# Two-layer decode step on one core: one load for the output weights of two head pairs, two pieces for the last values, four pieces for the last down weights

## Chip, cores and metric

One core of one Trainium2 chip. The metric is the device time of one execution in microseconds (us). A run is one execution.

## The reference

Two identical layers (the same weights) of attention and a gated MLP, for one token:

```python
x = x + A(layernorm(x)); x = x + B(layernorm(x))      # layer 0
x = x + A(layernorm(x)); x = x + B(layernorm(x))      # layer 1
# A: 32 heads of 192, keys and values: the last 4096 of 32768 positions, D = 640
#    q = x @ wq; p = softmax(q k^T * 192**-0.5); A = (p v) @ wo
# B: g = x @ w_gate; u = x @ w_up; B = (sigmoid(g) * u) @ w_down,  F = 1536
```

All inputs are bfloat16. The work is matrix times vector, so each byte of keys, values and weights is used once per layer, and the kernel is a stream of loads with a little computing beside it.

## The kernel before

The heads are handled in 16 pairs. For a pair, the host lays the projection weights and the keys in one unit ("a") and the values and the output weights in another ("b"); slots in on-chip memory hold 7 units. A list `seq` gives the order of the loads; all go out on one queue (SP), and each waits until the slot it writes is free. PE runs its instructions in order.

What the change touches, with cuts:

```python
WFIN = [(0, 6), (6, 10), (10, 12)]           # last down weights: chunks of each piece
def last_values(l, p):                       # last pair of a layer: values in three pieces
    return [("b1", l, p), ("b0", l, p, 0), ("b0", l, p, 1)]
seq = ... + [("a", 0, 15), ("b", 0, 14)] + last_values(0, 15)
seq += [("wol", 14), ("wol", 15)] + [(k,) for k in (*MW, *MV)] + ...   # MW: pieces of the MLP's weights
...
seq += [("fg",), ("fu",), ("fd", 0), ("fd", 1), ("fd", 2)]             # last MLP's weights
...
# down-weight pieces d0, d1 of layer 0's MLP overwrite gate pieces, so they are issued
# only after the gate projection has read those:
MAFTER = {"d0": ("wg0",), "d1": ("wg1",), ...}
...
# end of layer 0's attention (p = 15), in PE's order:
PVmm(p, 1)          # probabilities times values
RS(1, 2)            # row sums
PVn(p - 1, 0)       # output weights of pair 14: 15 matmuls, waits for load "wol14"
PVt(1, False)       # transpose pair 15's output: 6 matmuls, then one DVE operation
PVn(p, 1)           # output weights of pair 15: 15 matmuls, waits for load "wol15"
...
# the end of the kernel: each chunk of down weights is four matmuls on four column groups
for i_, (c0, c1) in enumerate(WFIN):
    for c in range(c0, c1):
        for g in range(NRG): matmul(yrow[32*g : 32*g+1, 0:RW], lhsT=hT[:, c:c+1], rhs=...)
```

## Time and profile before

| | |
|---|---|
| time, 3 runs | 515.14 us median (514.93 to 515.77) |
| span of the profiled run | 513.6 us |
| loads, read from the trace's packet records | 66 DMAs of 128 packets, 218.63 MB |
| last byte of weights landed | 510.72 us of the span |

From the profile's page, kernel before: the span; the DMA engines' busy share in tenths and the GB/s in 40 slices of the span; the queue of the loads (packets, MB, share of 16 engines' span); the chain that ended last by engine.

```profile
span 513.6 us, 8573 instructions
...
DMA  9999999999999999999999999999999999999996
GB/s 430 425 422 425 426 429 439 451 443 425 429 425 434 426 443 451 435 425 429 411 416 417 410 438 435 433 425 427 453 443 434 434 429 429 426 430 423 426 427 276
...
q1 hardware_dynamic: 9512, 218.63, 99.1%
...
DMA 63%; PE 24%; DVE 7%; ACT 2%; SPq 2%; issue 2%; DVEq 0%; POOL 0%; ACTq 0%; POOLq 0%
```

The DMA engines are full in every slice but the last, and most of the chain is DMA. PE, busy 51% on the page, waits for loads. A gain must come from the stream or from what follows its last byte. One weakness of the busy share: a packet that takes longer than usual counts as busy for all of its time. Slices 20 to 23 (about 244 to 295 us) show 410 to 417 GB/s, where the others but the last show 422 to 453, and the share does not show it.

The end of layer 0's attention, kernel before, from the timeline. Columns: start us, duration us, engine, line, operation, output<-input, shape, count, and in brackets the idle time before and what ended it. L502 applies output weights, L488 transposes, L377 is the residual sum that ends the attention, L212 issues loads.

```profile
271.20 0.54 PE L502 MATMUL bank<-sh,big 128*128 128x1 bf16 x15
...
271.80 0.30 PE L488 MATMUL bank<-cst,o_sb 128*128 128x1 bf16 x6
272.13 0.22 DVE L491 TENSOR_SCALAR sh<-bank,sc 128x3 bf16<-128x3 f32 x1 [0.48 <-PE bank L488]
...
272.63 0.56 PE L502 MATMUL bank<-sh,big 128*128 128x1 bf16 x15 [0.54 <-DMA big<-in_uc_dram]
273.23 0.16 DVE L377 SCALAR_TENSOR_TENSOR sc<-bank,sc 128x5 f32<-128x5 f32 x1 [0.87 <-PE bank L502]
...
274.95 0.90 SPq L212 DMA_DIRECT2D big<-in_wd_dram  x2
```

Pair 14's weights are applied at 271.20, then pair 15's output is transposed, and only then does PE wait 0.54 us, for pair 15's weights. The first down-weight load of the MLP is issued at 274.95.

The chain of waits at the end, kernel before (start us, duration us, what):

```profile
486.16 24.89 DMA big<-in_wd_dram
...
511.09 0.46 PE o L719 x7
...
511.57 0.33 DVE o_sb L725
```

The long DMA entry is the last load, issued at 486 us behind everything else. After it there are 0.46 us of matmuls and then the cast of the result.

### The profile page before, as it was taken

The numbers are of one execution on the slowest core, as the hardware profiler recorded it, in microseconds if no ns is written. First come the engines' busy times: TensorE is split into PE (matmuls) and PEld (weight loads), VectorE is DVE, ScalarE is ACT, GpSimd is POOL, SyncE is SP. The second block draws the span as 40 slices with busy tenths as digits, with TensorE's granted clock in tenths as the row PEclk, the third lists the DMA queues.
The fourth block names the chain that finished last, engine by engine and source line by source line (L and its number), as shares of the span: only waits on it lengthen the run. The fifth ranks groups of instructions, "written<-read, shape, count | busy, mean of one in ns | idle before, by whom it ended". The sixth has DMA issues, their size and how long they took to land.

```text
span 513.6 us, 8573 instructions
## 1 busy us (share of the span) xinstructions
PE 263.4 (51%) x3716; PEld 137.6 (27%) x3716; DVE 99.2 (19%) x376; ACT 85.2 (17%) x171; POOL 4.2 (1%) x31
## 2 busy tenths in 40 slices
PE   0462456344643265345566767864625245634665
PEld 0221222122311132222234434432312122212334
DVE  0221212112211121111121333231202112210311
ACT  0110111011110111011120033130301011101220
POOL 0010000000000000000000000000000000000000
PEclk9955665565566755566575568676857555556655
DMA  9999999999999999999999999999999999999996
GB/s 430 425 422 425 426 429 439 451 443 425 429 425 434 426 443 451 435 425 429 411 416 417 410 438 435 433 425 427 453 443 434 434 429 429 426 430 423 426 427 276
DMA packets 9676, 218.97 MB, mean 426 GB/s; under 512 B 1208, under 2 KB 1208, under 8 KB 4664
## 3 DMA queue, kind: packets, MB, share of 16 engines
q1 hardware_dynamic: 9512, 218.63, 99.1%
q8 instruction: 13, 0.21, 0.1%
q10 hardware_dynamic: 144, 0.06, 0.0%
q14 instruction: 7, 0.06, 0.0%
HBM read 218.69 MB, written 0.00 MB: 426 GB/s over the span
## 4 chain that ended last, share of the span: by engine, by line
DMA 63%; PE 24%; DVE 7%; ACT 2%; SPq 2%; issue 2%; DVEq 0%; POOL 0%; ACTq 0%; POOLq 0%
DMA big<-in_uc_dram 54%; PE scores L410 8%; PE o L467 7%; DMA big<-in_wd_dram 6%; DVE sc L420 3%; DMA big<-in_wu_dram 3%; PE bank L426 2%; SPq L212 2%; PE bank L395 2%; PE bank L502 1%; ACT e_sb L434 1%; PE bank L440 1%; ACT diag L423 1%; DVE sc L452 1%; DVE qs L398 1%
## 5 line engine op out<-in xcount | busy, mean ns | idle before, releaser
L410 PE MATMUL scores<-big,qs 128*32 128x512 bf16 x744 | 81.5, 605 | 9.9 <-DVE qs L398 9.9
L395 PE MATMUL bank<-sh,big 128*128 128x1 bf16 x465 | 17.1, 166 | 133.0 <-DMA big<-in_uc_dram 130.7
L467 PE MATMUL o<-big,et_sb 128*2 128x384 bf16 x1024 | 78.7, 474 | 5.9 <-DMA big<-in_uc_dram 3.4
L423 ACT ACTIVATE diag<-cst,sc 128x128 f32<-128x128 bf16 x32 | 12.8, 402 | 307.5 <-DVE sc L420 299.4
L420 DVE TENSOR_REDUCE sc<-scores 128x1 f32<-128x1024 f32 x31 | 38.0, 1225 | 79.2 <-PE scores L410 79.2
L395 PEld LDWEIGHTS bank<-sh,big 128*128 128x128 bf16 x465 | 14.6, 103 | 136.2 <-DMA big<-in_uc_dram 113.4
L426 PE MATMUL bank<-diag,sc 128*128 128x128 f32 x64 | 22.5, 447 | 47.9 <-ACT diag L423 47.9
L434 ACT ACTIVATE e_sb<-scores,sc 128x1024 bf16<-128x1024 f32 x31 | 37.4, 1205 | 41.8 <-DVE sc L429 39.5
L467 PEld LDWEIGHTS o<-big,et_sb 128*2 128x2 bf16 x1024 | 28.0, 108 | 43.8 <-issue 31.1
L398 DVE TENSOR_TENSOR qs<-bank,cst 128x96 bf16<-128x96 f32 x31 | 8.0, 258 | 162.4 <-PE bank L395 162.4
L410 PEld LDWEIGHTS scores<-big,qs 128*32 128x32 bf16 x744 | 23.7, 131 | 43.0 <-issue 29.6
L426 PEld LDWEIGHTS bank<-diag,sc 128*128 128x128 f32 x64 | 14.1, 274 | 73.0 <-ACT diag L423 71.5
L474 ACT CAST o_sb<-o 128x384 bf16<-128x384 f32 x64 | 29.8, 474 | 22.5 <-PE o L467 22.3
L502 PE MATMUL bank<-sh,big 128*128 128x1 bf16 x480 | 17.2, 165 | 15.2 <-DVE sh L491 14.6
L444 DVE CAST et_sb<-bank 128x64 bf16<-128x64 f32 x32 | 7.2, 225 | 71.8 <-PE bank L440 71.8
L502 PEld LDWEIGHTS bank<-sh,big 128*128 128x128 bf16 x480 | 14.5, 99 | 17.7 <-DVE sh L491 12.1
L427 DVE TENSOR_REDUCE sc<-bank 128x2 f32<-128x128 f32 x32 | 9.3, 292 | 42.1 <-PE bank L426 42.1
L440 PE MATMUL bank<-cst,e_sb 128*128 128x8 bf16 x256 | 11.7, 169 | 6.8 <-ACT e_sb L434 6.7
L440 PEld LDWEIGHTS bank<-cst,e_sb 128*128 128x128 bf16 x256 | 8.9, 101 | 22.9 <-issue 16.4
L450 PE MATMUL o<-sc 128*128 128x2 f32 x62 | 14.0, 295 | 0.6 <-ACT o_sb L474 0.6
L450 PEld LDWEIGHTS o<-sc 128*128 128x128 f32 x62 | 12.1, 243 | 1.9 <-ACT o_sb L474 1.3
L452 DVE RECIPROCAL sc<-o 64x1 f32<-64x1 f32 x62 | 10.2, 164 | 9.5 <-PE o L450 7.8
(76 smaller groups left out, 106.4 us busy)
## 6 DMA issues: line engine op xcount, KB each, us to landing
big<-in_uc_dram SPq DMA_DIRECT2D x20, 7104.0 KB, 22.6
big<-in_uc_dram SPq DMA_DIRECT2D x12, 3552.0 KB, 21.2
big<-in_uc_dram SPq DMA_DIRECT2D x1, 3072.0 KB, 21.5
big<-in_uc_dram SPq DMA_DIRECT2D x4, 768.0 KB, 11.6
big<-in_uc_dram SPq DMA_DIRECT2D x5, 480.0 KB, 6.9
big<-in_uc_dram SPq DMA_DIRECT2D x1, 2048.0 KB, 10.7
big<-in_uc_dram SPq DMA_DIRECT2D x1, 2016.0 KB, 10.6
big<-in_wg_dram SPq DMA_DIRECT2D x4, 480.0 KB, 14.7
```

The source lines that it names most:

```text
L395: ins = t.matmul(qe[:, i:i + 1], lhsT=slot(sa, c * 2 * DH + c0, P), rhs=xq[:, c:c + 1], start=(c == 0), stop=(c == DC - 1))
L410: ins = t.matmul(sc_x[1 + b][32 * j:32 * j + 32, :], lhsT=qs[:, y, k, :], rhs=slot(sa, WQE + k * W + (4 * b + j) * 512, 512), start=(k == ...
L420: pg.op("dve", lambda v: v.reduce_max(out=mx, in_=sc_x[0][:], axis=AX.X), wr=[res("mx")], ex=sc_x[3:5])
L423: pg.op("act", lambda a: a.mul(out=diag[:], in_=ident, mul=mx), rd=[res("cst"), res("mx")], wr=[res("diag")])
L426: pg.op("pe", lambda t: t.matmul(dmx[:, 0:P], lhsT=ones_f, rhs=diag[:], start=True, stop=True), rd=[res("diag"), res("ones")], ex=[rb[2]])
L434: pg.op("act", lambda a: a.activation(out=e_sb[:], in_=sc_x[0][:], func=ACT.Exp, bias=nbias, scale=srs_c, accum_out=rowsum), rd=[res("nbia ...
L440: ins = t.matmul(qe[:, 0:2 * NB].rearrange("p (r x) -> p r x", r=2)[:, :, 4 * b:4 * b + 4], lhsT=e_sb[:, b * P:(b + 1) * P], rhs=sel, star ...
L450: pg.op("pe", lambda t: t.matmul(sm, lhsT=ones_f, rhs=rs2[z], start=True, stop=True), rd=[res(f"rs2{z}"), res("ones")], wr=[res("rsum")], ...
L452: rb[bk].last["dve"] = pg.op("dve", lambda v, h=h: v.reciprocal(out=Rn[z][64 * h:64 * h + 64], in_=sm[64 * h:64 * h + 64, h:h + 1]), rd=[r ...
L467: ins = t.matmul(o8[h][32 * j:32 * j + 2, 0:2 * DH].rearrange("p (a d) -> p a d", a=2), lhsT=et_sb[:, z, h * NB + 2 * u:h * NB + 2 * u + 2 ...
L474: pg.op("act", lambda a, h=h: a.copy(out=o8_sb[:, :, h * DH:(h + 1) * DH], in_=o8[h][:, 0:2 * DH].rearrange("p (a d) -> p a d", a=2)), wr= ...
L502: ins = t.matmul(yT[:, j:j + 1], lhsT=wo[:, c * D + j * P:c * D + (j + 1) * P], rhs=oTb[z][:, c:c + 1], start=False, stop=(c == 2), skip_g ...
```

## The change

The intent: fewer, longer loads in the stream, and less work after the last byte. Output weights of pairs 14 and 15 get a buffer of their own and land as one row across the border of two neighbouring slots. Of the last values of a layer, the second head and half of the first come as one load, the last quarter follows. The last down weights come in four pieces, the last with one chunk instead of two.

```diff
-    WFIN = [(0, 6), (6, 10), (10, 12)]
+    WFIN = [(0, 6), (6, 10), (10, 11), (11, 12)]
     def last_values(l, p):
-        return [("b1", l, p), ("b0", l, p, 0), ("b0", l, p, 1)]
+        return [("b1", l, p), ("b0", l, p)]
-    seq += [("wol", 14), ("wol", 15)] + ...
+    seq += [("wol",)] + ...
-            pg.dma(q_dma(slot(s, NB * DH, o1 - NB * DH), b_in(it[2], NB * DH, o1)), f"b1_{it[1]}", wr=[rslot[s]])
+            pg.dma(q_dma(slot(s, NHALF, o1 - NHALF), b_in(it[2], NHALF, o1)), f"b1_{it[1]}", wr=[rslot[s]])
-            pg.dma(q_dma(slot(s, o, WOE), b_in(it[1], o, o + WOE)), f"wol{it[1]}", ...)
+            pg.dma(q_dma(big[:, PLACE[s] * UNIT + wo_at(15):PLACE[s] * UNIT + UNIT + WOE], wl_d), "wol", ...)
-                for part in (0, 1) if half and h == 0 else (None,):
+                for part in (1, 0) if half and h == 0 else (None,):
-                rw = [rslot[sv], res(f"wol{p}")]
+                rw = [rslot[sv], res("wol")]
... (waits and start/stop flags of the split values, the list entries of the last down weights, and the host's layout of the new buffer, are cut)
```

Bytes and matmuls stay the same; 66 loads become 64.

More of the change, by code (lines that the diff above doesn't have):

```diff
@@ L108, in decode_kernel @@
 def decode_kernel(ctx: ExitStack, nc, cx: bass.AP, uc: bass.AP,
-                  wg_d: bass.AP, wu_d: bass.AP, wd_d: bass.AP, out: bass.AP):
+                  wg_d: bass.AP, wu_d: bass.AP, wd_d: bass.AP, wl_d: bass.AP, out: bass.AP):
     scale = float(DH) ** -0.5
@@ L225, in last_values @@
     def last_values(l, p):
-        return [("b1", l, p), ("b0", l, p, 0), ("b0", l, p, 1)]
+        return [("b1", l, p), ("b0", l, p)]
     seq = [("a", 0, 0)] + [("c", 0, p) for p in range(1, 15)] + [("a", 0, 15), ("b", 0, 14)] + last_values(0, 15)
-    seq += [("wol", 14), ("wol", 15)] + [(k,) for k in (*MW, *MV)] + [("a0", 0), ("wom",), ("a0", 1), ("a0", 2), ("a", 1, 3), ("b", 1, 2)]
+    seq += [("wol",)] + [(k,) for k in (*MW, *MV)] + [("a0", 0), ("wom",), ("a0", 1), ("a0", 2), ("a", 1, 3), ("b", 1, 2)]
     seq += [("b", 1, 3), ("a", 1, 4), ("b", 1, 4), ("a", 1, 5), ("a", 1, 6), ("b", 1, 5)]
     seq += [("c", 1, p) for p in range(7, 13)] + [("a", 1, 13), ("b", 1, 12)] + last_values(1, 13)
-    seq += [("fg",), ("fu",), ("fd", 0), ("fd", 1), ("fd", 2)]
+    seq += [("fg",), ("fu",), *(("fd", i) for i in range(len(WFIN)))]
     seq_pos = [0]
@@ L284, in try_load @@
             s = B_SLOT[it[1]][it[2]]
-            o = it[3] * NHALF
-            pg.dma(q_dma(slot(s, o, NHALF), b_in(it[2], o, o + NHALF)), f"bh{it[3]}", wr=[res(f"bh{it[3]}")], extra=ev_done["b1"])
+            pg.dma(q_dma(slot(s, 0, NHALF), b_in(it[2], 0, NHALF)), "bh0", wr=[res("bh0")], extra=ev_done["b1"])
         elif k == "a0":
@@ L294, in try_load @@
         elif k == "wol":
-            s = B_SLOT[0][it[1]]
-            o = wo_at(it[1])
-            pg.dma(q_dma(slot(s, o, WOE), b_in(it[1], o, o + WOE)), f"wol{it[1]}", wr=[res(f"wol{it[1]}")], extra=ev_done["b1" if it[1] == 15 else "b14"])
+            s = B_SLOT[0][15]
+            assert PLACE[B_SLOT[0][14]] == PLACE[s] + 1 and wo_at(15) + WOE == UNIT and wo_at(14) == 0
+            pg.dma(q_dma(big[:, PLACE[s] * UNIT + wo_at(15):PLACE[s] * UNIT + UNIT + WOE], wl_d), "wol", wr=[res("wol")], extra=ev_done["b1"] + ev_done["b14"])
         elif k in MW:
@@ L460, in PVmm, with f @@
                 vt = (mreg(h * NB * DH, NB * DH) if inm else slot(sv, v_at(p) + h * NB * DH, NB * DH)).rearrange("p (t d) -> p t d", t=NB)
-                for part in (0, 1) if half and h == 0 else (None,):
+                for part in (1, 0) if half and h == 0 else (None,):
                     us = range(NB // 2) if part is None else range(part * NB // 4, (part + 1) * NB // 4)
-                    def f(t, h=h, vt=vt, us=us):
+                    first = range(NB // 4, NB // 4 + 4) if part is not None else range(4)
+                    final = range(NB // 4 - 4, NB // 4) if part is not None else range(NB // 2 - 4, NB // 2)
+                    def f(t, h=h, vt=vt, us=us, first=first, final=final):
                         for u in us:
@@ L467, in f @@
                             ins = t.matmul(o8[h][32 * j:32 * j + 2, 0:2 * DH].rearrange("p (a d) -> p a d", a=2), lhsT=et_sb[:, z, h * NB + 2 * u:h * NB + 2 * u + 2],
-                                           rhs=vt[:, 2 * u:2 * u + 2, :], start=(u < 4), stop=(u >= NB // 2 - 4), tile_position=(0, 32 * j))
+                                           rhs=vt[:, 2 * u:2 * u + 2, :], start=u in first, stop=u in final, tile_position=(0, 32 * j))
                         return ins
-                    rV = rc if inm else [rslot[sv]] + ([] if part is None else [res(f"bh{part}")]) if half else [rval[sv]]
+                    rV = rc if inm else [rslot[sv]] + ([res("bh0")] if part == 0 else []) if half else [rval[sv]]
                     ev = pg.op("pe", f, rd=[res(f"et{z}")] + rV, ex=[rb[4 + h]])
@@ L897, in _layout @@
     cx[:, C_X:] = x.reshape(DC, P).T
-    return dict(cx=cx, uc=uc, wg=blk(wg), wu=blk(wu), wd=wdn)
+    wl = np.concatenate([wo[n * 2 * DH:(n + 1) * 2 * DH].reshape(P, WOE) for n in (NPAIR - 1, NPAIR - 2)], axis=1)
+    return dict(cx=cx, uc=uc, wg=blk(wg), wu=blk(wu), wd=wdn, wl=wl)
 def kernel(**inputs):
```

## The prediction

> **What bounds the kernel.** The DMA stream. The page shows DMA at 9 tenths in every slice but the last, q1 at 99.1% of 16 engines' span, 426 GB/s; PE is busy 51%. The trace's packet records show no hole in q1 from about 2 us after the span's start until the last down weights. Their durations are very regular: 2,560 B 102 ns, 3,840 B 149, 7,680 B 291, 56,832 B 2,098. From these I estimate 27.2 B/ns per engine plus 8 ns per packet; a DMA also has a 9 ns semaphore packet. 27.2 x 16 = 435 GB/s, which the Trainium skill ("DMA: Bandwidth & Descriptors", "Where 436 GB/s comes from") gives as the port ceiling: the trace agrees. So only the packets' fixed part and the tail after the last byte can be saved; the bytes do not change.
>
> **The stream.** Removed: one DMA of last values per layer (2), one of output weights (1). Added: one of down weights. Net -2 DMAs, each costing an engine 8 packets x 8 ns + 9 ns = 73 ns (estimate): -0.15 us. The new 1,280 B packets should take 55 ns, by the same line. (The same page, "Why small descriptors are slow", names a fixed overhead per packet; the trace agrees in kind, with 8 ns.)
>
> **The tail.** In the trace the last piece's eight matmuls run as two waves of four, from 511.09 and 511.18 us; the cast follows at 511.57 (the chain of waits puts 0.46 us on them). With one chunk last there is one wave, 0.29 us per matmul: -0.15 us. Cast, output DMA and clears stay.
>
> **What gets worse but should be hidden.** In layer 0, PE, which is in order, applies the weights of pair 14 before it transposes pair 15's output. Now both pairs wait for one DMA, which lands when that of pair 15 did (PE idle 0.54 us on a DMA before the last 15 matmuls at 272.63, in the timeline). So pair 14's 0.55 us, the transposes' 0.3 us and DVE's 0.22 us come after the landing: layer 0's attention ends about 1.1 us later. That delays the first projections, and the issue of the first two down-weight pieces. Those start moving 2.75 and 3.85 us after issue; the kernel's first load needed 1.0. So about 1.7 us of slack takes 1.1 us of delay, and the projection then catches up (it idles 0.6 us per piece on landings). The last values: h=1 and half of h=0 (24 matmuls, about 1.3 us) start when the larger piece lands and end before the last quarter lands, some 1.8 us later; eight matmuls follow that, as before. In layer 1 the final weights are already queued, so nothing of this is on the chain.
>
> **Prediction.** 515.14 - 0.15 - 0.15 = about 514.8 us, range 514.2 to 515.4. Faster by over 2%: 0.005; within 2%: 0.985; slower: 0.01.
>
> **What would show it right.** Span about 0.3 us shorter; no hole in q1 at 275 to 285 us; 1,280 B packets near 55 ns; one wave of four matmuls between last landing and cast; layer 0's residual about 1 us later, with no effect on the end.
>
> **What would make it wrong.** The 1.1 us delay exceeds the slack and opens a hole in the stream (up to +1 us); small last packets land late; one DMA engine runs behind the others by another amount (the last piece starts over 2.7 us apart on different engines); or scatter (514.93 to 515.77 before) hides it all.

## The result, and the profile after

| | before | after |
|---|---|---|
| median of 6 runs each | 515.03 us (514.58 to 515.87) | 514.71 us (514.58 to 516.82) |
| ratio | | 0.9997, 95% interval 0.9979 to 1.0015 |

A ratio is the mean time of one kernel's runs over that of the other's of the same rounds, so it is not quite the ratio of the medians. The two kernels are the same at this resolution. Five of the six runs after lie between 514.58 and 514.75; the sixth, 516.82, is the one that was profiled.

The page's lines of that long run after, which answer those of before:

```profile
span 515.4 us, 8570 instructions
...
DMA  9999999999999999999999999999999999999996
GB/s 424 428 420 423 429 428 454 441 428 423 428 429 437 446 432 437 423 437 428 422 416 393 382 443 427 425 433 434 453 424 437 437 428 428 446 428 411 433 423 275
...
q1 hardware_dynamic: 9224, 218.63, 99.0%
...
DMA 64%; PE 24%; DVE 7%; ACT 2%; issue 2%; SPq 1%; DVEq 0%; ACTq 0%
```

The same lines of a short profiled run of the same kernel (514.57 us, from the experiments below, run again2):

```profile
span 513.3 us, 8570 instructions
...
DMA  9999999999999999999999999999999999999996
GB/s 426 430 422 425 422 435 430 447 447 430 430 425 425 439 425 434 452 438 434 402 415 413 413 439 438 428 433 434 440 430 452 438 430 425 435 430 421 427 429 276
...
q1 hardware_dynamic: 9224, 218.63, 99.2%
```

All DMA shares are alike. The long run differs in slices 22 and 23 (about 270 to 296 us), where the rate falls to 393 and 382 GB/s. These slices hold the MLP of layer 0.

The end of layer 0's attention, after, short run (L503 is before's L502, L489 before's L488, L376 before's L377):

```profile
272.55 0.54 PE L503 MATMUL bank<-sh,big 128*128 128x1 bf16 x15 [1.27 <-DMA big<-in_wl_dram]
...
272.95 0.30 PE L489 MATMUL bank<-cst,o_sb 128*128 128x1 bf16 x6
273.29 0.22 DVE L492 TENSOR_SCALAR sh<-bank,sc 128x3 bf16<-128x3 f32 x1 [1.61 <-PE bank L489]
...
273.57 0.56 PE L503 MATMUL bank<-sh,big 128*128 128x1 bf16 x15 [0.32 <-DVE sh L492]
274.17 0.16 DVE L376 SCALAR_TENSOR_TENSOR sc<-bank,sc 128x5 f32<-128x5 f32 x1 [0.66 <-PE bank L503]
...
275.90 0.81 SPq L212 DMA_DIRECT2D big<-in_wd_dram  x2
```

and three of these instructions in the long run:

```profile
273.31 0.51 PE L503 MATMUL bank<-sh,big 128*128 128x1 bf16 x15 [2.34 <-DMA big<-in_wl_dram]
...
274.89 0.17 DVE L376 SCALAR_TENSOR_TENSOR sc<-bank,sc 128x5 f32<-128x5 f32 x1 [0.64 <-PE bank L503]
...
276.62 0.80 SPq L212 DMA_DIRECT2D big<-in_wd_dram  x2
```

PE now waits on the row before pair 14's weights, and transposes, DVE and pair 15's weights follow one after the other behind that landing. The residual starts at 274.17 in the short run, 0.94 us later than before, and the first down-weight load is issued 0.95 us later. In the long run they are 1.66 and 1.67 us later than before.

The end of the chain of waits, long run after:

```profile
487.96 24.98 DMA big<-in_wd_dram
...
512.98 0.33 PE o L720 x4
...
513.34 0.32 DVE o_sb L726
```

Four matmuls, 0.33 us, stand where 0.46 us stood.

Three readings used below come from the trace's records, not from a view.
- The *lead* of the first down-weight load (piece d0 of layer 0's MLP) is the time from the start of its issue to the start of its first data packet. The Trainium skill ("Perfetto Trace Analysis", DMA Instruction, HWDGE) says that a DMA instruction's interval does not contain the movement of data; the trace agrees (two issues took 0.90 us together, and the first packet came 2.75 us after the first began), so the packets must be looked at.
- The *loss* at 270 to 300 us is, over all packets of the load queue, the duration beyond what a packet of its size usually takes, plus the time with fewer than 16 packets in flight, divided by 16 engines. It depends a little on how such packets are counted: a second count by these words gave 0.07 to 0.15 us more for every profile, with nearly the same ranking. Splits of the loss by time, below, are from the second count.
- The *period* is the time from the start of one packet to the start of the next on one engine, after sorting the packets to engines by size and by gapless succession.

### The profile page after: what moved, and what is told of

Read it like the earlier page. It is cut to its first block, busy times and chain, and to the rows that moved or that the text cites. A ratio compares the mean times of both kernels' runs of the same rounds, so it can differ in the third digit from the quotient of the medians. Undisturbed runs are those within 1.5% of the kernel's fastest.

```text
span 515.4 us, 8570 instructions
## 1 busy us (share of the span) xinstructions
PE 261.4 (51%) x3716; PEld 137.3 (27%) x3716; DVE 99.4 (19%) x376; ACT 84.7 (16%) x171; POOL 4.2 (1%) x31
## 3 DMA queue, kind: packets, MB, share of 16 engines
q1 hardware_dynamic: 9224, 218.63, 99.0%
## 4 chain that ended last, share of the span: by engine, by line
DMA 64%; PE 24%; DVE 7%; ACT 2%; issue 2%; SPq 1%; DVEq 0%; ACTq 0%
DMA big<-in_uc_dram 54%; PE scores L409 8%; PE o L468 7%; DMA big<-in_wd_dram 6%; DMA big<-in_wu_dram 4%; DVE sc L419 3%; PE bank L425 2%; PE bank L394 2%; PE bank L503 1%; SPq L212 1%; ACT diag L422 1%; ACT e_sb L433 1%; PE bank L439 1%; DVE sc L451 1%; DVE qs L397 1%
## 5 line engine op out<-in xcount | busy, mean ns | idle before, releaser
L409 PE MATMUL scores<-big,qs 128*32 128x512 bf16 x744 | 82.7, 612 | 10.0 <-DVE qs L397 9.9
L468 PE MATMUL o<-big,et_sb 128*2 128x384 bf16 x1024 | 75.7, 463 | 3.8 <-DMA big<-in_uc_dram 2.8
L468 PEld LDWEIGHTS o<-big,et_sb 128*2 128x2 bf16 x1024 | 27.6, 106 | 39.8 <-issue 30.0
L503 PE MATMUL bank<-sh,big 128*128 128x1 bf16 x480 | 17.2, 165 | 17.7 <-DVE sh L492 15.3
L503 PEld LDWEIGHTS bank<-sh,big 128*128 128x128 bf16 x480 | 14.6, 99 | 20.2 <-DVE sh L492 13.0
```

Of the source, the lines that this page charges most:

```text
L409: ins = t.matmul(sc_x[1 + b][32 * j:32 * j + 32, :], lhsT=qs[:, y, k, :], rhs=slot(sa, WQE + k * W + (4 * b + j) * 512, 512), start=(k == ...
L468: ins = t.matmul(o8[h][32 * j:32 * j + 2, 0:2 * DH].rearrange("p (a d) -> p a d", a=2), lhsT=et_sb[:, z, h * NB + 2 * u:h * NB + 2 * u + 2 ...
L503: ins = t.matmul(yT[:, j:j + 1], lhsT=wo[:, c * D + j * P:c * D + (j + 1) * P], rhs=oTb[z][:, c:c + 1], start=False, stop=(c == 2), skip_g ...
```

## The experiments

Theories. A is the prediction: a little less DMA overhead, a shorter tail, and a later end of layer 0's attention that is hidden. B: the row opens a hole in the stream of layer 0's MLP. C, formed after the first four runs: the later end of the attention eats the lead of the first down weights; when the lead is gone, there is a hole (a stretch in which the DMA engines move fewer bytes, because they are idle or their packets are lengthened). Two experiment kernels and the unedited one were run twice or more, to pool.

| run | what it is | median us (lowest to highest), runs | before, same rounds | residual us | lead us | loss us |
|---|---|---|---|---|---|---|
| profile before | | | | 273.23 | 2.75 | 0.49 |
| profile after (516.82) | unedited | 514.71 (514.58 to 516.82), 6 | 515.03 | 274.89 | 1.02 | 2.05 |
| again | unedited | 514.98 (514.44 to 515.29), 5 | 514.84 | 274.46 | 1.64 | 0.80 |
| again2 | unedited | 514.58 (514.36 to 515.76), 6 | 514.87 | 274.17 | 1.98 | 0.42 |
| row_only | before + the row | 514.98 (514.60 to 515.39), 5 | 514.84 | 274.24 | 1.78 | 0.58 |
| tail_only | before + four down pieces | 514.57 (514.47 to 515.25), 5 | 514.84 | 273.26 | 2.77 | 0.36 |
| vals_only | before + values in two pieces | 514.59 (514.45 to 515.18), 5 | 514.95 | 273.25 | 2.71 | 0.22 |
| no_row | changed, without the row | 514.57 (514.35 to 515.20), 5 | 514.95 | 273.11 | 2.82 | 0.18 |
| no_row2 | the same again | 514.76 (514.66 to 514.88), 5 | 514.87 | 273.32 | 2.76 | 0.48 |
| order15 | changed, PE order exchanged | 514.86 (514.40 to 515.68), 5 | 514.95 | 273.68 | 2.34 | 0.27 |
| order15_2 | the same again | 514.85 (514.40 to 514.89), 5 | 514.87 | 273.60 | 2.83 | 0.18 |
| row_late | changed, the row 2.3 us later | 517.04 (516.26 to 517.21), 5 | 514.95 | 276.88 | 0.96 | 2.32 |
| gate12 | changed, gate weights in 12 loads | 515.51 (514.64 to 515.93), 5 | 514.84 | 274.15 | 1.71 | 0.61 |

The last three columns come from the one profiled run of each. All results were correct.

### again, again2: the change once more, unedited

> The changed kernel once more, unedited, because its profiled run (516.82 us) was 2 us longer than its five others (514.58 to 514.75). Theory A (the gain is 0.15 us of DMA overhead and 0.15 us of PE tail; the later end of layer 0's attention is hidden): most runs 0.2 to 0.4 us under before, and the profile of a short run shows the first down-weight piece of the MLP of layer 0 moving no less than 1.0 us after its issue, and no lengthened packets at 276 to 297 us. Theory B (the one-row load opens a hole in the stream of layer 0's MLP, now and then): at least one run in six again 1.5 us or more above the shortest, and lengthened packets at 276 to 297 us in any profile of such a run; before then has no run that long.

> The unedited changed kernel a third time, beside the two candidates, to pool runs: single runs scatter by 1 us and the differences looked for are 0.2 us. Theory C: loss at 270 to 300 us of 0.6 us per engine or more in its profile, some runs over 515.2; median at or above those of the two candidates.

Measured: medians 514.98 and 514.58, so the first was 0.14 us over before and the second 0.29 us under. One run of the eleven reached 515.76, a second 515.29; none came near 516.82. But before reached 515.87, 515.77 and 515.66 as well. The expected "one in six" long runs of theory B did not come, nor in again the 0.2 to 0.4 us under before of theory A. Of again2's three expectations one held, a run over 515.2; its loss was 0.42, not 0.6 or more, and its median lay under both candidates'. So time alone does not tell these kernels apart. The lead, however, was 1.64 and 1.98 us, below 2.75 both times, and no profile without the row showed a lead below 2.7.

### row_only, tail_only, vals_only: each part alone

row_only is the row's lines of the diff above on the kernel before, tail_only the line `WFIN` and its loop, vals_only the lines of `last_values` and of the parts.

> Only the output weights of pairs 14 and 15 as one row. Theory A: one DMA less, 0.07 us under before; attention of layer 0 ends 1.1 us later, with no effect on the end. Theory B: the occasional long run (1.5 us and more) comes with this part alone, and the median is not under before.

> Only the last down weights in four pieces. Theory A: -0.15 us of PE tail + 0.07 us for one DMA more = 0.08 us under before; four matmuls in one wave of 0.29 us between last landing and cast. A rival, that the number of DMAs costs nothing and only bytes count: 0.15 us under before. Theory B: no long runs here, since the one-row load is not in it.

> Only the last values of a layer in two pieces, on the kernel before. Two DMAs less: 0.09 us under before. 24 matmuls in layer 0 (about 1.2 us) start when the larger piece lands and end before the last quarter lands; the end of the attention is not later; lead 2.7 us.

row_only: 514.98, 0.14 us over before of the same rounds; the interval of the ratio is 0.9993 to 1.0020, so this sign is not settled. The residual moves by 1.01 us and the lead shrinks to 1.78. That the delay belongs to the row is shown.

tail_only: 514.57, 0.27 us under before by medians (interval of the ratio 0.9985 to 1.0012, so not settled). In its trace the first of PE's weight loads for the last piece starts 0.358 us before the cast, against 0.488 before. Every profile with four pieces shows 0.354 to 0.358, every profile with three 0.487 or 0.488: the tail's gain is 0.13 us.

vals_only: 514.59, 0.36 us under before by medians, interval 0.9982 to 1.0009. The residual is not later (273.25 against 273.23). Its timeline at the last values (L468: probabilities times values):

```profile
268.09 2.73 PE L468 MATMUL o<-big,et_sb 128*2 128x384 bf16 x32 [1.59 <-DMA big<-in_uc_dram]
...
269.93 0.17 PEld L468 LDWEIGHTS o<-big,et_sb 128*2 128x2 bf16 x8 [0.47 <-DMA big<-in_uc_dram]
```

The 24 matmuls start at 268.09, and the weight loads for the last 8 wait 0.47 us on a landing: the larger piece is worked off in time.

### gate12: what a DMA costs in the full stream

```diff
@@ -314 +314,4 @@
-            pg.dma(q_dma(mreg(0, 12 * FW), wg_d), "fg", wr=rc)
+            for i in range(12):
+                ev = pg.dma(q_dma(mreg(i * FW, FW), wg_d[:, i * FW:(i + 1) * FW]), "fg", wr=[] if i else rc)
+            for r in rc:
+                r.w = ev
```

> The changed kernel with the last gate weights (1,920 KB) in 12 DMAs in place of one, to magnify the cost of a DMA elevenfold; same bytes. Theory A (73 ns per DMA: 8 packets x 8 ns + 9 ns): 0.80 us over the changed kernel. Rival (only bytes count): no difference. A third, that it is the queue's issue of 0.45 us each: hidden too, as the issues run 15 us ahead, so no difference.

Measured: 515.51 against 514.98 of the unedited change in the same rounds, 0.53 us for 11 DMAs, 48 ns each. The ratio of gate12 to the kernel before has the interval 1.0002 to 1.0029, so there is a cost, but its size is loose, and the profiled run, at 514.64, shows none of it in its total time. Its packets show it: from the first packet of the last gate weights to the first of the last down weights it took 9.60 us, and 9.12 us in all twelve other profiles, 0.48 us for 11 DMAs. The periods say where that goes. On one engine a packet of 1,280 B is followed by the next after 52 ns, one of 3,840 B after 146, one of 7,680 B after 287, one of 56,832 B after 2,094: 4.8 ns plus 0.03676 ns per byte. Where the next packet belongs to the next DMA, it comes about 6 ns later. The duration of a packet is 3 ns longer than its period, as each starts before the one in front has ended, and that is what the prediction overlooked. A DMA costs an engine 8 x 4.8 + 6 = 44 ns (an estimate from these periods), not 73 ns; 11 make 0.49 us, near the 0.48 of the packets and the 0.53 of the medians. The rivals, that only bytes count or that the issue hides it, do not fit the packets or the periods.

### row_late: a larger dose of the delay

```diff
@@ -228 +228 @@
-    seq += [("wol",)] + [(k,) for k in (*MW, *MV)] + [("a0", 0), ("wom",), ("a0", 1), ("a0", 2), ("a", 1, 3), ("b", 1, 2)]
+    seq += [("wg0",), ("wg1",), ("wol",)] + [(k,) for k in (*MW, *MV) if k not in ("wg0", "wg1")] + [("a0", 0), ("wom",), ("a0", 1), ("a0", 2), ("a", 1, 3), ("b", 1, 2)]
```

> The changed kernel with the one-row load queued behind the first two gate pieces, 2.3 us later; bytes and DMAs the same. A larger dose of the same delay. Theory C: the lead of the first down weights falls to the 1.0 us that an idle engine needs, loss at 270 to 300 us at least 1.5 us per engine, and the median 0.8 to 2.5 us over the unedited changed kernel. Theory A (slack hides it): no difference.

Measured: 517.04 against 514.95 of before, every run above 516.2. The timeline, row_late:

```profile
275.26 0.54 PE L503 MATMUL bank<-sh,big 128*128 128x1 bf16 x15 [3.93 <-DMA big<-in_wl_dram]
...
276.88 0.16 DVE L376 SCALAR_TENSOR_TENSOR sc<-bank,sc 128x5 f32<-128x5 f32 x1 [0.66 <-PE bank L503]
...
278.61 0.80 SPq L212 DMA_DIRECT2D big<-in_wd_dram  x2
```

The residual moves to 276.88 and the down weights are issued at 278.61; the first packet comes 0.96 us after. The first load of the kernel, on idle engines, took 1.01 to 1.05 us in all profiles, so here the engine that moved it first had run dry when the load was issued. The view of busy time by stretch, for 270 to 285 us (columns: stretch and length in us; busy us and count of PE, PE's weight loads, DVE, ACT and POOL; the granted clock; DMA share; GB/s), kernel before:

```profile
270.00:285.00 15.00, 9.00 (x200) 7.37 (x200) 2.12 (x15) 1.21 (x4) 0.00 (x0) 0.50 1.02 416
```

The same, row_late:

```profile
270.00:285.00 15.00, 6.88 (x175) 6.04 (x175) 1.89 (x14) 1.23 (x5) 0.00 (x0) 0.65 0.93 360
```

The same, the long run after:

```profile
270.00:285.00 15.00, 7.15 (x175) 6.14 (x175) 1.89 (x14) 1.21 (x4) 0.00 (x0) 0.65 1.00 385
```

At 15 us, 416 against 360 and 385 GB/s are bytes worth 2.0 and 1.1 us at before's rate (15 x 56 / 416 and 15 x 31 / 416) that move later. For row_late theory C is shown: the later row takes the lead, and all five runs are longer, where theory A expected no difference.

The long run after resembles row_late in lead (1.02 against 0.96), loss (2.05 against 2.32) and span (515.4 against 515.1), but not in when the loss comes. The same view in shorter stretches, row_late:

```profile
276.00:281.00 5.00, 4.11 (x114) 3.97 (x114) 0.93 (x9) 0.70 (x3) 0.00 (x0) 0.50 0.77 285
281.00:285.00 4.00, 1.26 (x36) 1.01 (x32) 0.63 (x3) 0.04 (x1) 0.00 (x0) 0.50 1.00 365
```

and the long run after:

```profile
276.00:281.00 5.00, 3.13 (x92) 3.00 (x93) 0.68 (x6) 0.73 (x3) 0.00 (x0) 0.50 1.01 385
281.00:285.00 4.00, 1.40 (x41) 1.15 (x38) 0.23 (x1) 0.00 (x0) 0.00 (x0) 0.50 0.95 342
```

In row_late the engines stand idle where the first down weights start (share 0.77), and 1.74 of 2.43 us are lost at 276 to 282 us. In the long run only 0.45 of 2.20 us are lost there, and 1.04 at 282 to 288 us, more than 4 us after the first down weights began to move, in later loads. Most of it is in lengthened packets and not in idle engines (1.71 us of the table's 2.05), which is why the share is 1.00 over the 15 us. So row_late shows that a lead of 1.0 us can go with a hole, and the profiles with leads of 1.6 to 2.0 lost 0.42 to 0.80 us. That the short lead caused all the loss of the long run is not shown.

### order15: the PE order exchanged

```diff
@@ -572,0 +573 @@
+            PVt(1, False)
@@ -574 +574,0 @@
-            PVt(1, False)
```

> The changed kernel with one pair of PE steps of layer 0 exchanged: pair 15's output is transposed before pair 14's weights are applied, so that only the 30 matmuls with the weights stand behind the one-row load. What is known by now: in the long profiled run (516.82 us) the first down-weight piece of the MLP moved 1.02 us after its issue, and lengthened packets and holes took 2.05 us per engine at 270 to 300 us of the span; with the row and a short run 1.64 to 1.78 us and 0.58 to 0.80; without the row 2.77 us and 0.36 to 0.49. Theory C (the row's later end of attention eats the lead of the first down weights, and what is lost there takes back a gain of about 0.2 us): lead back at 2.1 to 2.4 us, loss at 270 to 300 us below 0.55, median 0.1 to 0.4 us under the unedited changed kernel's (514.71 and 514.98 so far), no long run. Rival (the loss there is chance, not the row): as the unedited changed kernel.

> The kernel with the exchanged PE steps again (514.86 before, with one run at 515.68; loss 0.27). Theory C: lead 2.1 to 2.4 us, loss 0.25 to 0.55, median between the other two. Rival: no order among the three that holds.

Its timeline (run order15):

```profile
271.82 0.30 PE L489 MATMUL bank<-cst,o_sb 128*128 128x1 bf16 x6 [0.54 <-DVE sc L451]
...
272.71 0.94 PE L503 MATMUL bank<-sh,big 128*128 128x1 bf16 x30 [0.58 <-DMA big<-in_wl_dram]
273.68 0.16 DVE L376 SCALAR_TENSOR_TENSOR sc<-bank,sc 128x5 f32<-128x5 f32 x1 [1.29 <-PE bank L503]
...
275.41 0.80 SPq L212 DMA_DIRECT2D big<-in_wd_dram  x2
```

Pair 15's output is now transposed before the landing, and 30 matmuls in one go (0.94 us) follow it. The residual is 0.45 and 0.37 us later than before instead of 0.94 or more; leads are 2.34 and 2.83, losses 0.27 and 0.18. The mechanism is as expected, though in order15_2 the lead was longer and the loss smaller than forecast. The medians are not: 514.86 and 514.85, no gain over the unedited change within the scatter (order15_2 lay above both it and no_row2, not between them), and one run at 515.68.

### no_row: the change without the row

Its edit is the change with the lines of `wol` as in the kernel before.

> The changed kernel with the output weights of pairs 14 and 15 in two DMAs again; values in two pieces and down weights in four as changed. By periods read from the traces a DMA costs an engine 44 ns (8 x 4.8 + 6), not 73. So -0.04 us of stream (one DMA less on balance) and -0.13 us of tail: 0.17 us under before. Theory C: lead 2.7 us, loss at 270 to 300 us 0.3 to 0.5, at or below the unedited changed kernel. Rival: 0.05 us over the unedited changed kernel, for the DMA more.

> The kernel without the one-row load again (514.57 before, loss 0.18). Theory C: loss 0.2 to 0.5, median 0.1 to 0.4 us under the unedited changed kernel of these rounds, and 0.17 us or more under before. Rival: no order among the three that holds.

Measured: 514.57 and 514.76, under before of the same rounds by 0.38 and 0.11 us; leads 2.82 and 2.76, losses 0.18 and 0.48. Of no_row2's expectations only the loss held: its median was 0.18 us over that of the unedited change, not 0.1 to 0.4 under, and less than 0.17 under before; its rival, no order among the three, stands. The same view for a short run of the unedited change (again2):

```profile
270.00:285.00 15.00, 8.66 (x200) 7.16 (x200) 2.09 (x15) 1.21 (x4) 0.00 (x0) 0.50 1.02 413
```

for order15:

```profile
270.00:285.00 15.00, 8.78 (x200) 7.25 (x200) 2.11 (x15) 1.21 (x4) 0.00 (x0) 0.50 1.02 414
```

and for no_row:

```profile
270.00:285.00 15.00, 8.76 (x200) 7.30 (x192) 2.11 (x15) 1.21 (x4) 0.00 (x0) 0.50 1.02 417
```

The rates, 413, 414 and 417 GB/s beside before's 416, differ by 1% at most: there is no hole.

Of the ten runs none was over 515.20; of the unedited change's 17 runs three were, of before's 25 runs four. Pooled over all rounds the medians are 514.89 (before, 25 runs), 514.67 (changed, 17), 514.76 (no_row, 10) and 514.86 (order15, 10); the means are 514.92, 514.89, 514.72 and 514.80. The candidate without the row has the lowest mean and the narrowest scatter, but no order among the four is settled.

## Why the prediction was right, and where its terms were off

The predicted time (514.8, measured 514.71) and "within 2%" were right. That says little by itself: the change forecast, 0.3 us, is smaller than the scatter of single runs, and that the medians of the first comparison lay 0.32 us apart is partly luck (again had 0.14 us the other way). The terms are what can be checked. Point by point:

1. *The DMA stream bounds the kernel.* Right. A count from the periods (estimate): 218.63 MB over 16 engines at 0.03676 ns per byte is 502.3 us per engine, with 528 packets x 4.8 ns and 66 x 6 ns 505.2 us, and the last byte lands at 510.72; the start (first packet at 1.01 us) and lengthened packets are not in the count. The 435 GB/s of the Trainium skill ("DMA: Bandwidth & Descriptors", Where 436 GB/s comes from) is what 0.03676 ns per byte and 16 engines give.
2. *Net two DMAs less, 73 ns each, -0.15 us.* Right in kind, mis-sized: a DMA costs 44 ns in the full stream, because consecutive packets overlap by 3 ns, so -0.09 us. The packets of gate12 show it.
3. *1,280 B packets take 55 ns.* Right: all 256 took 55 ns.
4. *The tail, -0.15 us.* Right; it measured -0.13 us (0.488 to 0.356 us from the first weight load for the last piece to the cast).
5. *Layer 0's attention ends 1.1 us later.* Right: the residual is 0.92 to 1.23 us later in the shorter profiled runs with the row (0.37 and 0.45 with the order exchanged, nothing without the row).
6. *1.7 us of slack takes it; no hole; the projection catches up.* Right for the shorter runs that were profiled: leads of 1.64 to 1.98 us were left, and the load of 7,680 B packets issued at about 283 us led by 2.56 us in again and 2.42 in again2, against 2.35 before. In the one long run that was profiled the delay was 1.66 us, the lead fell to 1.02, and a hole came, about 2 us where the prediction's first danger said "up to +1"; most of it came later than that danger says (see row_late). The slack was read from one profile and treated as fixed (and the second piece's 3.85 us is too long: by the records it began to move about 3.35 us after its own issue). The attention ended another 0.7 us later in that run because the completion of the row's load was signalled late, not its data: the last data packet ended at 272.09 us (again2: 271.96), the last of the 16 semaphore increments came at 273.18 (again2: 272.42). An 8 KB packet of the page's queue q14 (kind "instruction") moved at 271.81 us, as the row ended; in the other profiles, row_late aside, it moved at 269.5 to 270.6. That it delayed the signal is not shown.
7. *The last values are worked off before the last quarter lands.* Right (vals_only).

What is shown: the tail's 0.13 us, the 44 ns, the delay by the row, that the exchanged order takes back more than half of it, and the hole when the row comes 2.3 us later still (row_late). What is not shown: that the change makes the kernel faster. The sum of the corrected terms is -0.22 us, the pooled medians differ by as much, the pooled means by 0.03, and the intervals (0.9979 to 1.0015 in the first comparison) are wider. Nor is it shown that the row costs time in a run without a hole: losses were 0.42, 0.58, 0.61 and 0.80 us with it (0.18 and 0.27 with the order exchanged), and 0.18 to 0.49 without, and these ranges overlap. What lengthened the packets of the long run after 282 us is open too. What makes single runs of the kernel before 1 us longer was not profiled.

## What to carry to other kernels

In a full DMA stream, merging loads saves little (44 ns per DMA here), while a merged load makes its first user wait for its last byte; look at which user stands first in an in-order engine, and move independent work ahead of it. A load issued late is safe only as long as its lead, read from the packets, stays above what an idle engine needs (1.0 us here); a change that shortens the lead may cost nothing that shows, and a little more delay then costs 2 us in every run (row_late). A profile taken in the odd run shows another story than the median, so take a second one before explaining the first.

## What the Trainium skill lacked or had wrong

- "DMA: Bandwidth & Descriptors", Measured, advises at least 1 MiB per DMA for 75% of peak, from transfers issued by GpSimd. For loads queued on SP behind others much smaller ones reach that here: 12 loads of 160 KB in place of one of 1,920 KB cost 0.48 us in the packet records, and the period of a 1,280 B packet, 52 ns, is 24.6 B/ns, 90% of the 27.2 that the 0.03676 ns per byte give. The page has no cost of one more DMA in a full queue: 44 ns here.
- The same page, Why small descriptors are slow (HBM only), gives the overhead per packet in cycles and bytes only; here the period has a fixed 4.8 ns per packet and about 6 ns more at a new DMA.
- The same page, Latency and other measured facts, gives about 600 ns to the first byte for this path. From the start of the issue to the first data packet on idle engines it was 1.01 to 1.05 us in all 13 profiles.
- "Perfetto Trace Analysis", DMA Engine Tracks, says that slices show actual busy time. In an underfed queue the packets' own durations grow: in the long run 1.71 of 2.05 us of loss were in lengthened packets and 0.34 in gaps, so a busy share of 1.00 stood beside 385 GB/s.
